# Attention regrouped, and 40 unused products ahead of the first transposes, in a chain of attention and two gated layers

## The chip, the core and the metric

One core of a Trainium2 chip. The time is the device time of one execution in microseconds (us); 0.2% of it, 3.4 us, is about what a measurement of this kernel can tell from no change. The engines are TensorE (PE for its products, PEld for the loading of its stationary operand), VectorE (DVE), ScalarE (ACT), GpSimd (POOL) and SyncE (SP), which issues all DMAs here. Each engine takes its instructions in the order in which the program lists them.

## The reference

```
kv  = einsum('bhsd,bhse->bhde', k, v)             # 8 batches, 8 heads, 576 tokens, 64
out = einsum('bhsd,bhde->bhse', q, kv)
x   = out / sqrt(mean(out*out, -1) + 1e-6) * g_norm   # to 4608 tokens x 512
x   = (sigmoid(x @ w_gate) * (x @ w_val)) @ w_out     # inner width 1536
x   = elu(x @ w_in) @ w_out2                          # inner width 2048
```

All is f32. The attention has no softmax: a 64 x 64 product of k and v per batch and head, and then q times it.

## The kernel before

**Blocks.** The 4608 tokens are cut into 12 blocks of 384 (three chunks of 128), and a batch has 576 tokens, so the border between two batches falls into the middle of a block in every third block (1, 4, 7, 10), and there one of its three chunks of 128 is split into two of 64. Blocks go in pairs (g = 0 to 5).

**Precision.** An f32 operand is split into a high and a low part (fp32r), and a product is three: high x high, high x low, low x high (matmul3, lines 425 to 427). The weights come from memory as raw 64-bit words and are decoded once: `decode` (line 279) loads two pieces of raw (512 KB each, line 288), works on them with ACT (290, 292) and DVE (294, 298), and then ACT writes the high part into a tile S (342) and DVE the low part (344). S, high and low, and the words (wf) are stored for later blocks.

**Attention of a block** (`attention`, line 458). If a batch is new, `kv_batch` (437) loads k and v in four pieces of 512 KB and a tail of 256 KB, multiplies them on PE (451, 453), and ACT copies the results into kvb (455). Then two tasks, each for two pairs of heads, multiply q with kvb (481); ACT squares (488), DVE sums up (489), 13 small DVE operations compute the inverse root (497 to 504), and DVE scales (516, the normalisation, four operations). PE transposes the result (526, four tasks of three), ACT writes the high part of x (533) and DVE the low part (534).

**First layer.** For blocks 0 and 1 `in1_plain` (618) makes, for a pair of inner tiles fp, four groups of 12 products: g for e = 0 and 1, v for e = 0 and 1. The calls are plain(0, 0), plain(1, 0), plain(0, 1), plain(1, 1), where the first number is fp and the second the block; then the other fp. Later pairs of blocks use a scheme with seven products in place of eight on sums and differences (`quad`, line 561); there the attention of the next pair is merged into the products of the present one.

**Second layer.** `in2` (685), and then the output: `out2_plain` (696) for the first pair of blocks, whose six results go through four tiles xp and from there to memory, and `out2` (716) for the five other pairs. `out2` first makes the differences T1, T2, T3 (`combine`, 723), eight operations each on POOL, and T4 on DVE; its products split each operand into a tile J with ACT (644) and DVE (646).

**What sets the order.** The PE order is written by hand (`plan.pe` and the lists `later`). All other work is put in order by a planner (`Plan`, line 60), which plays the program with its own costs and gives each engine the work that is due next; buffers come from pools of fixed size (`slots`: five S, three raw, four wk, three kv, one tail, four xp, 48 v, and eight product banks, psi and psa). A DMA that is issued waits for the one that was issued eight before.

The start before: attention of block 0, then the products of batch 1's k and v (line 818), then the transposes of block 0, then plain(0, 0) with block 1's attention products between its g and v groups, plain(1, 0), the transposes of block 1, plain(0, 1).

The functions that the diff touches:

Of the kernel before, what the change touches and what calls it, by code (L numbers as in the profile page):

```python
# [9 lines left out]
F32 = mybir.dt.float32  # L10
# [11 lines left out]
P = 128  # L22
# [4 lines left out]
BLK = 384  # L27
# [195 lines left out]
def tile_kernel(ctx: ExitStack, tc: tile.TileContext, kv, kvtail, qt, g2, w1, w2, out):  # L223
# [213 lines left out]
    def kv_batch(b, queue, first=False, bank="psa"):  # L437
        tl = plan.buf("tail")
        ld_t = dma(P * 2048, lambda: nc.sync.dma_start(out=tl.slot, in_=kvtail[b]), bufs=[tl], early=30.0)
        for p in range(NP):  # L440
            t, view, ld = load_kv(b, p, "wk" if first and p > 1 else "kv")
            pb = plan.buf(bank)

            def mm(t=t, view=view, pb=pb, p=p):

                k, r = view(), slice(p % 2 * D, p % 2 * D + D)
                for c in range(SC + 1):
                    for h in range(2):
                        e = slice(h * D, h * D + D)
                        if c < SC:  # L450
                            nc.tensor.matmul(pb.slot[e, :D], k[:, 0, c, e], k[:, 1, c, e], start=(c == 0), stop=False)  # L451
                        else:
                            nc.tensor.matmul(pb.slot[e, :D], tl.slot[r, p // 2, 0, e], tl.slot[r, p // 2, 1, e], start=False, stop=True)
            m = add("PE", 0.98, mm, [ld, ld_t], [t, tl, pb], queue=queue)
            kvdone[b, p] = [add("ACT", 0.2, lambda pb=pb, p=p, e=slice(h * D, h * D + D): nc.scalar.activation(
                kvb[b % 2][e, p, e], pb.slot[e, :D], AF.Copy), [m] + kvread.get((b - 2, p), []), [pb]) for h in range(2)]

    def attention(j, queue, direct=None, bank="psa", gap=3, hold=None):
# [8 lines left out]
        for pp in range(NP // 2):  # L467
            qs, lds = [], []
            for p in (2 * pp, 2 * pp + 1):
                qb = plan.buf("v", "q")  # L470
                lds.append(dma(P * BLK * 4, lambda qb=qb, p=p: nc.sync.dma_start(out=qb.slot, in_=qt[j, p]), bufs=[qb], early=30.0))
                qs.append(qb)
            o, x = [plan.buf(bank) for _ in range(2)], plan.buf("xp")

            def mm(qs=qs, o=o, pp=pp):

                for k in range(2):
                    for i in range(TPB):
# [4 lines left out]
            m = add("PE", 0.9, mm, lds + sum((kvdone[b, p] for b in bs for p in (2 * pp, 2 * pp + 1)), []), qs + o, queue=queue)  # L483
# [30 lines left out]
        for pp in range(NP // 2):  # L514
            for h in range(2):
                norm[pp, h] = add("DVE", T_DVE, lambda x=xn[pp], o=po[pp][h], pp=pp, h=h: nc.vector.tensor_tensor(
                    x.slot[:, h, :].rearrange("q (n d) -> q n d", d=D), o.slot[:, :BLK].rearrange("q (n d) -> q n d", d=D),
                    small(2)[:, 2 * pp + h, :].unsqueeze(2).to_broadcast([P, 2 * TPB, D]), op=ALU.mult), last, [xn[pp], po[pp][h], sm])
        for p in range(NP):
            x, n = xn[p // 2], [norm[p // 2, p % 2]]  # L520
            tp = plan.buf("psa")

            def tr(x=x, tp=tp, p=p):
                v = x.slot[:, p % 2, :].rearrange("q (i n) -> q i n", n=P)
                for i in range(TPB):
                    nc.tensor.transpose(tp.slot[:, i * P:(i + 1) * P], v[:, i, :], ident)  # L526
            m = add("PE", 0.35, tr, n, [x, tp], queue=queue)
            if direct is None:
                f = plan.buf("v", "xf")
                res.append((f, add("ACT", T_ACT, lambda f=f, tp=tp: nc.scalar.activation(f.slot, tp.slot[:, :BLK], AF.Copy, scale=gcol), [m], [tp, f])))  # L530
            else:
                f, c = direct[p // 2], p % 2
                hi = add("ACT", T_ACT, lambda f=f, c=c, tp=tp: nc.scalar.activation(f.slot[:, c, 0, :], tp.slot[:, :BLK], AF.Copy, scale=gcol), [m], [tp, f])
                res.append((f, [hi, add("DVE", T_DVE, lambda f=f, c=c, tp=tp: nc.vector.scalar_tensor_tensor(  # L534
                    f.slot[:, c, 1, :], tp.slot[:, :BLK], gcol, f.slot[:, c, 0, :].bitcast(F32), op0=ALU.mult, op1=ALU.subtract), [hi], [tp, f])]))
        return res


# [76 lines left out]

        return {(0, 0): res["11"], (0, 1): res["12"], (1, 0): res["21"], (1, 1): res["22"]}

    def in1_plain(fp, blk, sg, dg, sv, dv, xs, dx, between=()):

        res = {}  # L620
        banks = {(w, e): plan.buf("psi") for w in "gv" for e in range(2)}
# [1 line left out]
        for w, s, d in (("g", sg, dg), ("v", sv, dv)):  # L623
            for e in range(2):
# [71 lines left out]
    def out2_plain(g, hs):  # L696
        acc = {blk: [plan.buf("psi" if blk == 0 else "psa") for _ in range(TPB)] for blk in range(2)}
        for f in range(NF2):
            if f % 2 == 0:
                s, ld = stream("O", f // 2)  # L700
            for blk in in_blocks(f, NF2):
                j, dj = split(*hs[f // 2][f % 2, blk])
                for i in range(TPB):
# [3 lines left out]
                                *v, f == 0, f == NF2 - 1)  # L707
                    t = add("PE", 3 * MMW, mm, ld + dj, [acc[blk][i], s, j])
                    if f == NF2 - 1:
                        e = plan.buf("xp")  # L710
                        view = lambda e=e: e.slot.rearrange("q a n -> q (a n)")[:, :DM]
                        c = copy_out(i, view, lambda b=acc[blk][i]: b.slot, [t], [e, acc[blk][i]])
                        r0 = (2 * g + blk) * BLK + i * P
                        dma(P * 2048, lambda view=view, r0=r0: nc.sync.dma_start(out=out[r0:r0 + P, :], in_=view()), [c], [e], due=0.5)

    def out2(g, hs):
# [6 lines left out]
        def combine(x, y, dst=None, eng="POOL"):  # L723
            res = []
            for i, ((a, da), (b, db)) in enumerate(zip(x, y)):
                d = dst[i][0] if dst else plan.buf("w")
                e, t = (nc.gpsimd, T_POOL) if eng == "POOL" else (nc.vector, T_DVE)
                t = add(eng, t, lambda e=e, d=d, a=a, b=b: e.tensor_tensor(d.slot, a.slot, b.slot, op=ALU.subtract),
                        [da, db] + used.get(d, []) + ([] if dst else [gate]), [d, a, b])
                for x in {a, b} - {d}:  # L730
                    used.setdefault(x, []).append(t)
# [92 lines left out]
    hs = [{} for _ in range(NF1 // 2)]  # L824
    xa, xb = [X0["x11"], X0["x21"]], [X0["x12"], X0["x22"]]

    def plain(fp, blk, between=()):
# [91 lines left out]
```

## Time and profile before

| | us |
|---|---|
| median of 3 runs | 1685.37 (1684.62 to 1686.62) |
| the profiled execution | 1685.98 |
| its span | 1684.2 |
| PE busy in it | 1657.7 |
| DVE, ACT, POOL busy | 1106.6, 813.4, 334.4 |

PE has almost no idle time in the middle of the kernel. In the first 100 us it is idle for 12.6 us, and the granted clock of TensorE is 0.95 on average there; in the rest it is at 1.00. A row of the timeline gives start, duration, engine, line, operation, what it writes and reads by the program's names without buffer numbers, the number of instructions, and in brackets the idle time before the first of them and what ended it.

### The profile page before, as it was taken

To read this page: it belongs to the slowest core of one execution; us is meant where nothing else is said; L and a number is where in the kernel's file an instruction comes from. 1 tells how busy PE (TensorE), PEld (TensorE's weight loads), DVE (VectorE), ACT (ScalarE), POOL (GpSimd) and SP (SyncE) were. 2 spreads that over 40 slices of the span, in tenths; PEclk is the share of its full clock that TensorE was granted. 3 is DMA by queue.
4 is the path that set the end of the run, shared out by engine and by line. 5 is a ranking of instruction groups with operands and counts; after the bars stand their busy time and mean duration, and the time that the engine had idled before them with its cause. 6 is when DMAs were issued, how large, how long until landed. Compare 5 with 4: busy or idle time off the path is not lost.

```text
span 1684.2 us, 28777 instructions
## 1 busy us (share of the span) xinstructions
PE 1657.7 (98%) x10759; PEld 1622.3 (96%) x10759; DVE 1106.6 (66%) x2054; ACT 813.4 (48%) x1663; POOL 334.4 (20%) x326
## 2 busy tenths in 40 slices
PE   8899999999999999999999999999999999999998
PEld 6899999999999999999999998899999999999998
DVE  5769467655764674567356688678678578568575
ACT  5556333543532343335235465456456456456454
POOL 0001355311311230122021000050140240330320
PEclk9999999999999999999999999999999999999999
DMA  8998887889778778776788899988778778778774
GB/s 318 333 314 297 325 309 273 319 295 327 266 248 291 287 272 291 276 256 244 244 303 330 284 341 334 323 287 296 249 279 285 255 266 297 253 267 290 252 266 161
DMA packets 134332, 480.04 MB, mean 285 GB/s; under 512 B 12080, under 2 KB 60720, under 8 KB 106032
## 3 DMA queue, kind: packets, MB, share of 16 engines
q1 hardware_dynamic: 134192, 478.20, 80.4%
q8 instruction: 85, 1.39, 0.3%
q14 instruction: 55, 0.45, 0.1%
HBM read 393.22 MB, written 84.93 MB: 284 GB/s over the span
## 4 chain that ended last, share of the span: by engine, by line
PE 95%; DVE 2%; DMA 1%; issue 1%; ACT 0%; SPq 0%; DVEq 0%
PE psi L425 21%; PE psi L426 21%; PE psi L427 21%; PE psi L755 4%; PE psi L753 4%; PE psi L754 4%; PE psa L426 4%; PE psa L427 4%; PE psa L425 4%; PE psa L481 2%; PE psa L754 2%; PE psa L753 2%; PE psa L755 2%; PE psa L451 1%; PE psa L526 1%
## 5 line engine op out<-in xcount | busy, mean ns | idle before, releaser
L577 DVE TENSOR_TENSOR v<-v,psi 128x384 f32<-128x384 f32 x540 | 297.5, 552 | 228.8 <-PE psi L427 217.8
L425 PE MATMUL psi<-x,S 128*128 128x384 f32 x1056 | 359.4, 340 | 3.0 <-DVE v L577 2.8
L427 PE MATMUL psi<-x,S 128*128 128x384 f32 x1056 | 354.5, 336 | 4.1 <-DVE S L344 4.1
L426 PE MATMUL psi<-x,S 128*128 128x384 f32 x1056 | 354.3, 335 | 0.2 <-DVE x L534 0.2
L644 ACT ACTIVATE J<-v 128x384 fp32r<-128x384 f32 x336 | 175.1, 523 | 234.2 <-PE psa L427 80.0
L646 DVE TENSOR_TENSOR J<-v,J 128x384 fp32r<-128x384 f32 x336 | 205.0, 617 | 126.0 <-ACT J L644 125.0
L425 PE MATMUL psi<-xt,S 128*128 128x384 f32 x648 | 220.0, 340 | 1.4 <-DVE v L577 1.3
L427 PE MATMUL psi<-xt,S 128*128 128x384 f32 x648 | 216.8, 335 | 0.0
L426 PE MATMUL psi<-xt,S 128*128 128x384 f32 x648 | 216.5, 334 | 0.0
L425 PEld LDWEIGHTS psi<-x,S 128*128 128x128 f32 x1056 | 199.3, 189 | 4.9 <-DVE v L577 3.9
L427 PEld LDWEIGHTS psi<-x,S 128*128 128x128 f32 x1056 | 199.0, 188 | 4.5 <-DVE S L344 4.5
L426 PEld LDWEIGHTS psi<-x,S 128*128 128x128 f32 x1056 | 199.1, 189 | 1.0 <-DVE x L534 0.8
L613 POOL TENSOR_TENSOR v<-v,v 128x384 f32<-128x384 f32 x90 | 98.6, 1102 | 392.9 <-DVE v L577 305.8
L755 PE MATMUL psi<-S,J 128*128 128x256 f32 x560 | 159.4, 285 | 5.1 <-DVE J L646 5.1
L753 PE MATMUL psi<-S,J 128*128 128x256 f32 x560 | 158.4, 283 | 0.0
L754 PE MATMUL psi<-S,J 128*128 128x256 f32 x560 | 158.4, 283 | 0.0
L690 ACT ACTIVATE v<-v 128x384 f32<-128x384 f32 x144 | 75.0, 521 | 128.6 <-DVE v L577 128.6
L692 DVE SCALAR_TENSOR_TENSOR v<-v,v 128x384 f32<-128x384 f32 x144 | 87.8, 610 | 58.8 <-ACT v L691 58.8
L425 PEld LDWEIGHTS psi<-xt,S 128*128 128x128 f32 x648 | 121.7, 188 | 3.4 <-DVE v L577 2.7
L426 PEld LDWEIGHTS psi<-xt,S 128*128 128x128 f32 x648 | 121.7, 188 | 0.0
L427 PEld LDWEIGHTS psi<-xt,S 128*128 128x128 f32 x648 | 121.6, 188 | 0.0
L755 PEld LDWEIGHTS psi<-S,J 128*128 128x128 f32 x560 | 107.4, 192 | 6.3 <-DVE J L646 6.1
(153 smaller groups left out, 3336.7 us busy)
## 6 DMA issues: line engine op xcount, KB each, us to landing
S<-wsO SPq DMA_DIRECT2D x78, 1024.0 KB, 6.2
S<-wsI SPq DMA_DIRECT2D x48, 1024.0 KB, 5.3
S<-wso SPq DMA_DIRECT2D x36, 1024.0 KB, 6.3
S<-wsI SPq DMA_DIRECT2D x48, 768.0 KB, 6.0
raw<-w SPq DMA_DIRECT2D x68, 512.0 KB, 6.4
S<-wsg SPq DMA_DIRECT2D x24, 1024.0 KB, 5.3
S<-wsv SPq DMA_DIRECT2D x24, 1024.0 KB, 5.1
S<-wsg SPq DMA_DIRECT2D x30, 768.0 KB, 6.3
```

Source lines behind the costliest of these rows:

```text
L425: nc.tensor.matmul(acc, wh, xh, start=first, stop=False, skip_group_check=more)
L426: nc.tensor.matmul(acc, wh, xl, start=False, stop=False, skip_group_check=more)
L427: nc.tensor.matmul(acc, wl, xh, start=False, stop=last, skip_group_check=more)
L577: return add("DVE", T_DVE, lambda: nc.vector.tensor_tensor(dst.slot, a.slot, bank[k].slot[:, :BLK], op=ALU.add), after, [dst, a, bank[k]])
L613: t = add("POOL", T_POOL, lambda r=r, b=b: nc.gpsimd.tensor_tensor(r.slot, r.slot, b.slot, op=ALU.mult), [d, s], [r, b])
L644: hi = add("ACT", T_ACT, lambda: nc.scalar.activation(j.slot[:, 0, :], f.slot, AF.Copy), [d], [j, f])
L646: lo = add("DVE", T_DVE, lambda: nc.vector.tensor_tensor(j.slot[:, 1, :], f.slot, j.slot[:, 0, :].bitcast(F32), op=ALU.subtract), [hi], [j ...
L690: a1 = add("ACT", T_ACT, lambda e=e, b=b: nc.scalar.activation(e.slot, ps_or_v(b), AF.Relu, scale=-1.0), [d], [e, b])
L692: res[int(n[0]) - 1, int(n[1]) - 1] = (e, add("DVE", T_DVE, lambda e=e, b=b: nc.vector.scalar_tensor_tensor(e.slot, e.slot, -1.0, ps_or_v( ...
L753: nc.tensor.matmul(acc, x[0], w[:, 0], start=st, stop=False, skip_group_check=True)
L754: nc.tensor.matmul(acc, x[0], w[:, 1], start=False, stop=False, skip_group_check=True)
L755: nc.tensor.matmul(acc, x[1], w[:, 0], start=False, stop=last and f == n - 1, skip_group_check=True)
```

## The change

Seven edits, all in the way the same results are computed:

1. The products of batch 1's k and v leave their place ahead of the first transposes and stand among the first block's products: plain(0, 0) has them after its two g groups, block 1's attention products after the first v group; block 1's transposes stand after the first v group of plain(1, 0). Batch 1's fourth piece of k and v goes through four v buffers in four DMAs.
2. 40 products of 256 columns (bf16, of the identity matrix) that nobody reads stand ahead of the first transposes.
3. In an attention task the whole chunks come first, and then the split ones.
4. The transposes are two tasks of six in place of four of three, each after both its normalisations.
5. The third results of out2_plain go through raw and tail in place of xp.
6. In `combine` the last of the eight operations is DVE's.
7. The planner counts 1.4 in place of 0.9 for an attention task on PE.

The core of the diff:

```diff
@@ kv_batch
-            t, view, ld = load_kv(b, p, "wk" if first and p > 1 else "kv")
+            if b == 1 and p > 2:
+                t = [plan.buf("v", "kvx") for _ in range(SC)]
+                chunk = lambda c, t=t: t[c].slot[:, :2 * P].rearrange("q (a n) -> q a n", a=2)
+                ld = [dma(P * 1024, ..., bufs=[t[c]], early=30.0) for c in range(SC)]
...
@@ attention
-                for k in range(2):
-                    for i in range(TPB):
+                whole = [len(spans(j * BLK + i * P, j * BLK + i * P + P)) == 1 for i in range(TPB)]
+                for k, i in [(k, i) for w in (True, False) for k in range(2) for i in range(TPB) if whole[i] == w]:
...
-        for p in range(NP):
-            x, n = xn[p // 2], [norm[p // 2, p % 2]]
-            tp = plan.buf("psa")
+        for pp in range(NP // 2):
+            x, tps = xn[pp], [plan.buf("psa") for _ in range(2)]
...
@@ in1_plain
-            plan.pe += between
-            between = ()
+                plan.pe += between.get(len(t), [])
@@ out2_plain
-                        e = plan.buf("xp")
+                        e, form = ((plan.buf("xp"), ...), (plan.buf("xp"), ...),
+                                   (plan.buf("tail"), ...) if blk else (plan.buf("raw"), ...))[i]
@@ combine
-                e, t = (nc.gpsimd, T_POOL) if eng == "POOL" else (nc.vector, T_DVE)
+                on = "DVE" if i >= n - 1 else eng
+                e, t = (nc.gpsimd, T_POOL) if on == "POOL" else (nc.vector, T_DVE)
@@ the start
-    ra = attention(0, main, [X0["x11"], X0["x21"]], gap=0, hold=later[0])
-    kv_batch(1, main, bank="psi")
-    main += later[0]
+    tr = []
+    ra = attention(0, main, [X0["x11"], X0["x21"]], gap=0, hold=tr)
+    spare = plan.buf("psi")
+
+    def idle_products():
+        z = ident.bitcast(BF16)
+        for _ in range(40):
+            nc.tensor.matmul(spare.slot[:, :256], z[:, :P], z, start=True, stop=True)
+    add("PE", 0.0, idle_products, [], [spare])
+    main += tr
+    kv_batch(1, later[0])
...
-    plain(0, 0, later[1])
-    plain(1, 0)
-    main += later[2]
+    plain(0, 0, {2: later[0], 3: later[1]})
+    plain(1, 0, {3: later[2]})
```

SP's queue at the very start, before (kv, tail and wk hold k and v, v the q tiles here):

```order
L813 DMA gcol_66<-g2 128x1 [waits Activation_49]
L435 DMA kv0_143<-kv 128x1024
L439 DMA tail0_146<-kvtail 128x512
L435 DMA kv1_144<-kv 128x1024
L435 DMA wk0_139<-kv 128x1024
L435 DMA wk1_140<-kv 128x1024
L471 DMA v0_80<-qt 128x384
```

The load of gcol stands first, and the four pieces of k and v in a row. And after:

```order
L435 DMA kv0_143<-kv 128x1024
L439 DMA tail0_146<-kvtail 128x512
L435 DMA kv1_144<-kv 128x1024
L435 DMA wk0_139<-kv 128x1024
L820 DMA gcol_66<-g2 128x1 [waits Activation_49]
L288 DMA raw0_136<-w1 128x1024
L288 DMA raw1_137<-w1 128x1024
L435 DMA wk1_140<-kv 128x1024
L477 DMA v0_80<-qt 128x384 [waits DMAHW0_49]
```

The load of gcol, which waits for ACT, moved behind four loads of k and v, and two raw weight loads stand ahead of the fourth.

DVE's queue around the normalisation of block 0 and the first low halves of x, after (the small operations of lines 503 to 510 are ahead of it; before, lines 294 and 298 stand behind the normalisation, line 516, and line 344 of the first tile stands between them and the low halves, line 534; now both steps of the first tile, S0, stand ahead of the first reduction):

```order
L294 SCALAR_TENSOR_TENSOR wk0_139<-raw0_136,wk0_139 128x512
L522 TENSOR_TENSOR xp0_76<-psa0_153,sm0_147 128x384
L522 TENSOR_TENSOR xp0_76<-psa1_154,sm0_147 128x384
L522 TENSOR_TENSOR xp1_77<-psa2_155,sm0_147 128x384
L522 TENSOR_TENSOR xp1_77<-psa3_156,sm0_147 128x384
L298 SCALAR_TENSOR_TENSOR wk1_140<-wk1_140,wk0_139 128x1024
L540 SCALAR_TENSOR_TENSOR x110_69<-psa0_153,gcol_66,x110_69 128x384
L540 SCALAR_TENSOR_TENSOR x110_69<-psa1_154,gcol_66,x110_69 128x384
```

The decode of the second tile (v of the first pair) has a step ahead of the normalisation and one between it and the low halves.

DVE's queue in the first call of out2, where the last inputs come from in2 (line 692 before, 697 after) and the first product's J (646, now 651) are made, before:

```order
L692 SCALAR_TENSOR_TENSOR v23_103<-v23_103,v10_90 128x384
L646 TENSOR_TENSOR J2_135<-v32_112,J2_135 128x384
L692 SCALAR_TENSOR_TENSOR v40_120<-v40_120,v11_91 128x384
L646 TENSOR_TENSOR J0_133<-v18_98,J0_133 128x384
L646 TENSOR_TENSOR J1_134<-v36_116,J1_134 128x384
L646 TENSOR_TENSOR J2_135<-v16_96,J2_135 128x384
```

And after, with the last operations of T1, T2 and T3 (line 735):

```order
L697 SCALAR_TENSOR_TENSOR v33_113<-v33_113,v41_121 128x384
L651 TENSOR_TENSOR J2_135<-v8_88,J2_135 128x384
L735 TENSOR_TENSOR kv0_143<-v33_113,v45_125 128x384
L697 SCALAR_TENSOR_TENSOR v40_120<-v40_120,v32_112 128x384
L651 TENSOR_TENSOR J0_133<-v36_116,J0_133 128x384
L735 TENSOR_TENSOR kv0_143<-v18_98,kv0_143 128x384
L651 TENSOR_TENSOR J1_134<-v5_85,J1_134 128x384
L735 TENSOR_TENSOR v33_113<-v18_98,v33_113 128x384
L651 TENSOR_TENSOR J2_135<-v43_123,J2_135 128x384
```

One combination stands ahead of the second of these J (J0) and one ahead of each of the two that follow.

## Rows read from the trace of the kernel before

**Rows 1.** The page: shares of the chain that ended last, by engine.

```profile
PE 95%; DVE 2%; DMA 1%; issue 1%; ACT 0%; SPq 0%; DVEq 0%
```

**Rows 2.** Stretches: us, busy time (instructions) by engine, granted clock, DMA share, GB/s.

```profile
0.00:6.50 6.50, 3.17 (x7) 0.89 (x7) 1.30 (x4) 1.49 (x2) 0.70 (x6) 1.00 0.39 126
6.50:13.40 6.90, 5.99 (x81) 4.91 (x81) 0.00 (x0) 1.31 (x6) 0.00 (x0) 1.00 1.02 384
...
18.30:21.00 2.70, 2.70 (x61) 2.23 (x60) 2.27 (x10) 1.36 (x5) 0.00 (x0) 1.00 1.04 416
21.00:25.00 4.00, 0.00 (x0) 0.00 (x0) 3.72 (x11) 3.81 (x8) 0.00 (x0) 0.94 0.89 335
25.00:29.00 4.00, 3.96 (x33) 3.73 (x33) 3.38 (x5) 2.42 (x6) 0.00 (x0) 0.50 0.79 268
...
48.40:51.80 3.40, 3.40 (x12) 3.40 (x11) 1.91 (x4) 1.55 (x2) 0.00 (x0) 0.50 1.01 343
58.50:100.00 41.50, 41.33 (x250) 40.91 (x249) 32.20 (x56) 25.97 (x46) 0.00 (x0) 1.00 0.91 331
160.00:200.00 40.00, 40.00 (x233) 40.00 (x232) 22.64 (x36) 17.77 (x30) 8.86 (x11) 1.00 0.96 365
```

**Rows 3.** Timeline, the first instructions of ACT and SP's issues.

```profile
0.73 1.28 ACT L801 ACT_TABLE_LOAD   x1 [0.73 <-PEq L912]
...
2.25 0.39 SPq L813 DMA_DIRECT2D gcol<-g  x1
...
14.36 1.46 SPq L288 DMA_DIRECT2D raw<-w  x3
```

**Rows 4.** Timeline of PE and DVE, 13 to 59 us.

```profile
13.40 4.97 PE L481 MATMUL psa<-kvb,v 128*128 128x128 f32 x24
...
22.19 1.95 DVE L516 TENSOR_TENSOR xp<-psa,sm 128x384 f32<-128x384 f32 x4
24.05 1.28 DVE L294 SCALAR_TENSOR_TENSOR wk<-raw,wk 128x512 int32<-128x512 int32 x2
25.44 1.23 DVE L298 SCALAR_TENSOR_TENSOR wk<-wk,wk 128x1024 int32<-128x1024 int32 x1
...
28.93 2.19 DVE L534 SCALAR_TENSOR_TENSOR x<-psa,gcol,x 128x384 fp32r<-128x384 f32 x4
...
34.50 4.20 PE L481 MATMUL psa<-kvb,v 128*128 128x128 f32 x32
38.46 0.42 PE L425 MATMUL psi<-x,S 128*128 128x384 f32 x1
...
44.24 1.95 DVE L516 TENSOR_TENSOR xp<-psa,sm 128x384 f32<-128x384 f32 x4
...
47.37 0.44 PE L427 MATMUL psi<-x,S 128*128 128x384 f32 x1 [4.14 <-DVE S L344]
...
57.04 1.47 PE L526 MATMUL psa<-ident,xp 128*128 128x128 f32 x12
58.27 0.42 PE L425 MATMUL psi<-x,S 128*128 128x384 f32 x1
```

**Rows 5.** Stretches of line 481 alone: a task with split chunks, one without.

```profile
226.44:228.38 1.94, 1.94 (x16) 1.36 (x16) 1.00 1.05 350
77.55:78.81 1.26, 1.26 (x12) 1.26 (x12) 1.00 1.04 416
```

**Rows 6.** Timeline of DVE and PE at the end of out2_plain.

```profile
1081.49 0.69 DVE L651 COPY xp<-psa 128x512 f32<-128x512 f32 x1 [4.57 <-DMA out<-xp]
...
1084.38 0.44 PE L425 MATMUL psi<-x,S 128*128 128x384 f32 x1 [2.56 <-DVE v L577]
```

**Rows 7.** Waits of PE, 1100 us on (total, times, longest); timeline at one of them.

```profile
PE psi L755 <- DVE J L646: 5.1, 5, 1.0
...
1619.57 1.03 POOL L728 TENSOR_TENSOR wk<-v,v 128x384 f32<-128x384 f32 x1 [3.31 <-DVE v L692]
1619.61 1.40 DVE L646 TENSOR_TENSOR J<-v,J 128x384 fp32r<-128x384 f32 x1
...
1625.21 0.56 DVE L646 TENSOR_TENSOR J<-v,J 128x384 fp32r<-128x384 f32 x1 [0.69 <-ACT J L644]
```

More of the change, by code (lines that the diff above doesn't have):

```diff
@@ L440, in kv_batch, with mm @@
         for p in range(NP):
-            t, view, ld = load_kv(b, p, "wk" if first and p > 1 else "kv")
+            if b == 1 and p > 2:
+                t = [plan.buf("v", "kvx") for _ in range(SC)]
+                chunk = lambda c, t=t: t[c].slot[:, :2 * P].rearrange("q (a n) -> q a n", a=2)
+                ld = [dma(P * 1024, lambda c=c, chunk=chunk: nc.sync.dma_start(out=chunk(c), in_=kv[b, p][:, :, c, :]), bufs=[t[c]], early=30.0) for c in range(SC)]
+            else:
+                t, view, ld = load_kv(b, p, "wk" if first and p > 1 else "kv")
+                t, ld, chunk = [t], [ld], lambda c, view=view: view()[:, :, c, :]
             pb = plan.buf(bank)
-            def mm(t=t, view=view, pb=pb, p=p):
-                k, r = view(), slice(p % 2 * D, p % 2 * D + D)
+            def mm(chunk=chunk, pb=pb, p=p):
+                r = slice(p % 2 * D, p % 2 * D + D)
                 for c in range(SC + 1):
@@ L450, in mm @@
                         if c < SC:
-                            nc.tensor.matmul(pb.slot[e, :D], k[:, 0, c, e], k[:, 1, c, e], start=(c == 0), stop=False)
+                            nc.tensor.matmul(pb.slot[e, :D], chunk(c)[:, 0, e], chunk(c)[:, 1, e], start=(c == 0), stop=False)
                         else:
                             nc.tensor.matmul(pb.slot[e, :D], tl.slot[r, p // 2, 0, e], tl.slot[r, p // 2, 1, e], start=False, stop=True)
-            m = add("PE", 0.98, mm, [ld, ld_t], [t, tl, pb], queue=queue)
+            m = add("PE", 0.98, mm, ld + [ld_t], t + [tl, pb], queue=queue)
             kvdone[b, p] = [add("ACT", 0.2, lambda pb=pb, p=p, e=slice(h * D, h * D + D): nc.scalar.activation(
@@ L482, in mm @@
                                              kvb[b % 2][:, 2 * pp + k, :], start=True, stop=True)
-            m = add("PE", 0.9, mm, lds + sum((kvdone[b, p] for b in bs for p in (2 * pp, 2 * pp + 1)), []), qs + o, queue=queue)
+            m = add("PE", 1.4, mm, lds + sum((kvdone[b, p] for b in bs for p in (2 * pp, 2 * pp + 1)), []), qs + o, queue=queue)
             for b in bs:
@@ L518, in attention @@
                     small(2)[:, 2 * pp + h, :].unsqueeze(2).to_broadcast([P, 2 * TPB, D]), op=ALU.mult), last, [xn[pp], po[pp][h], sm])
-        for p in range(NP):
-            x, n = xn[p // 2], [norm[p // 2, p % 2]]
-            tp = plan.buf("psa")
[L523 to L535, printed above, removed]
@@ new lines, in attention, with tr @@
+        for pp in range(NP // 2):
+            x, tps = xn[pp], [plan.buf("psa") for _ in range(2)]
+            def tr(x=x, tps=tps):
+                for n, tp in enumerate(tps):
+                    for i in range(TPB):
+                        nc.tensor.transpose(tp.slot[:, i * P:(i + 1) * P], x.slot[:, n, i * P:(i + 1) * P], ident)
+            m = add("PE", 0.62, tr, [norm[pp, 0], norm[pp, 1]], [x] + tps, queue=queue)
+            for c, tp in enumerate(tps):
+                if direct is None:
+                    f = plan.buf("v", "xf")
+                    res.append((f, add("ACT", T_ACT, lambda f=f, tp=tp: nc.scalar.activation(f.slot, tp.slot[:, :BLK], AF.Copy, scale=gcol), [m], [tp, f])))
+                else:
+                    f = direct[pp]
+                    hi = add("ACT", T_ACT, lambda f=f, c=c, tp=tp: nc.scalar.activation(f.slot[:, c, 0, :], tp.slot[:, :BLK], AF.Copy, scale=gcol), [m], [tp, f])
+                    res.append((f, [hi, add("DVE", T_DVE, lambda f=f, c=c, tp=tp: nc.vector.scalar_tensor_tensor(
+                        f.slot[:, c, 1, :], tp.slot[:, :BLK], gcol, f.slot[:, c, 0, :].bitcast(F32), op0=ALU.mult, op1=ALU.subtract), [hi], [tp, f])]))
@@ L709, in out2_plain @@
                     if f == NF2 - 1:
[L710 to L711 removed]
+                        e, form = ((plan.buf("xp"), "q a n -> q (a n)"), (plan.buf("xp"), "q a n -> q (a n)"),
+                                   (plan.buf("tail"), "q a b n -> q (a b n)") if blk else (plan.buf("raw"), "q a b -> q (a b)"))[i]
+                        view = lambda e=e, form=form: e.slot.bitcast(F32).rearrange(form)[:, :DM]
                         c = copy_out(i, view, lambda b=acc[blk][i]: b.slot, [t], [e, acc[blk][i]])
@@ L825, in tile_kernel, with plain @@
     xa, xb = [X0["x11"], X0["x21"]], [X0["x12"], X0["x22"]]
-    def plain(fp, blk, between=()):
+    def plain(fp, blk, between={}):
         r, xs = (ra, xa) if blk == 0 else (rb, xb)
```

4 lines of the change are left out of this document (2 added, 2 removed).

## The prediction

> **What bounds the kernel now.** I read the chain of waits by engine first: TensorE (PE) stands on 95% of it [rows 1]. So time is gained only where PE stands still, runs at its lower clock, or does work that needn't be done. The table of stretches then says where that is. In 160 to 200 us PE is never idle and a product of 384 columns takes 40.00/233 = 0.172 us; the first 58 us look otherwise: nothing at all on PE in 21 to 25 us, a granted clock of 0.50 in 25 to 29 us and again in 48.4 to 51.8 us [rows 2]. Loads run at 384 GB/s from 6.5 us on. The timeline names the second gap: at 47.37 PE had waited 4.14 us for the low half of a decoded weight tile (S, line 344) [rows 4], which stands on VectorE (DVE) behind the whole normalisation of the second block. Last, the waits of the later stages: one of 2.56 us at 1084 us [rows 6], and five of 1.0 us, one in each of the five last output stages [rows 7].
>
> **1. The start, up to the first product of plain(0, 1), which stands at 58.27 us [rows 4].** Before, the first load waits behind that of gcol, issued at 2.25, when ScalarE's (ACT) table load from 0.73 and its first instruction are over [rows 3]. Now four loads stand ahead of gcol and wait for nothing, so the stream can begin at about 0.75, 1.5 to 1.9 us earlier. But two raw weight loads (1 MiB) stand ahead of the fourth kv load. By an estimate from the rates of [rows 2], 0.82 MB are there at 6.5 and 384 GB/s follow; up to the fourth kv load it is now 3.41 MB, which is 13.25 less 1.9 = 11.4 us, and with the q loads 4.19 MB, 13.4 us; loads that are open together finish out of turn, for which I add 0 to 1.3 us. The fourth kv product costs twice the 0.88 us that a step has at full clock (2.70 us for three [rows 2]). So the first block's attention products start between 13.4 (as before [rows 4]) and 14.7; I take 14.1, 0.7 later than before.
>
> From there every step is moved by 0.7: the products (4.97 us) end at 19.0, and the four normalisations, which began at 22.19, could begin at 22.9. Now DVE has one decode step in front of them (half of 1.28, so 0.64): 23.5; they take 1.95, to 25.4; another decode step (1.23) ends at 26.6, and the four low halves of x follow in steps of 2.19/4 = 0.55 [rows 4]: 27.2 to 28.8. The idle products (40 of 256 columns, by columns 256/384 of 0.172 = 0.115 us each, 4.6 us in all) run from 19.0 to 23.6 while PE would wait anyway; the transposes can start after two normalisations at 24.4. If they run at the lower clock for some time they end later, but up to about 25.6 the decode step in front of the low halves covers it; 9.2 us, all of them at half clock, would cost 2.6. The transposes themselves (12, 1.23 us at full clock) are hidden under DVE too. The weight chain for the first product no longer bounds: its raw loads, issued at 14.36 before [rows 3], are now the sixth and seventh of the stream, and its DVE steps stand ahead of the first reduction.
>
> First product of the first weight pair: held by the low halves, done two products after 28.8, 29.15. Then PE has no reason to wait: second product group 12 x 0.172 = 2.06, 31.2; the kv products that stood in the gap now cost 4 x 0.88 and a little for entering, 3.6, 34.8; third group 36.9; attention of block 1, 3.96 before (34.50 to its end 38.46) and 0.5 less by the regrouping below, 40.4; fourth 42.5; three groups of the second weight pair 48.7; 12 transposes 49.9; the last group 52.0. The moved kv products bring seven loads with them; the tail's waits in SP's queue for the last products of batch 0, as it did before, and by the counting of bytes (7.6 MB) all are there at 24, before 31.2. Their copies on ACT stand among decode steps of 0.5 to 1.1 us and are wanted at 36.9, two us after the last. Is the weight there in time? The second pair's first tile was 4.14 us late because DVE took the normalisation first; in the order of after it stands ahead of the second reductions, and by the same counting is ready near 37, five us before 42.5. The normalisation of block 1 came 44.24 + 1.95 - 38.46 = 7.7 us after the attention products; now 48.1, just ahead of 48.7. Result: 58.27 - 52.0 = **6.3 us** gained. Bounds: 7.5 with loads as early as they can be; 2.0 with two stretches at half clock (below), the normalisation a us late, and a later decode late by 1 to 2, for loads run at a share of 0.91 in 58 to 100 us [rows 2] and everything now asks for them earlier.
>
> At one place the Trainium skill speaks against the idle products. The row first: 25 to 29 us holds kv products and the first transposes, and the granted clock stayed at 0.50 (1.2 GHz) to its end although PE was busy for 3.96 of 4.00 us [rows 2]. The Trainium skill, TensorE: Matmul & The Clock Gate, section Part 4: PE-mode transpose, says that transposes do not count as PE being busy as other products do; by it the transposes after the idle products would not hold the clock up, and the sum would be the rival "clock" below. The row agrees with it, but the clock had already fallen there; that it falls in such a place no row shows.
>
> **2. Regrouped attention products.** Only blocks with a split chunk change: 1, 4, 7, 10. A task with two split chunks takes 1.94 us and one without takes 1.26 [rows 5], so a split chunk costs 0.34 more than a whole one. Now both split chunks stand together, and one entry and one exit go. Bounds 0 and 0.34 a task; I take 0.25, since the products themselves remain. Six tasks outside the start: **1.5 us** (0 to 2.0). Transposes in pairs issue the same instructions; nothing is to be had there, since PE does not wait at them in the middle of the kernel.
>
> **3. Copies at the end of out2_plain.** Six copies into four xp tiles: DVE's copy waited 4.57 us for a store out of xp, DVE's later sums stood behind it, and PE waited 2.56 us for one of them [rows 6]. With raw and tail as third targets no copy waits for a store. Tail is loaded no more by then, and of raw's three tiles the sums of the output weights, off PE's path, want one; the sum that PE waited for can follow its products at once, and nothing else is seen late there: **2.6 us** (0 to 2.7).
>
> **4. The last combination of each three on DVE instead of POOL.** Five times PE waits 1.0 us for a low half J [rows 7]. The rows say why: beside a POOL operation (1619.57, 1.03 us) DVE's step on two such tiles takes 1.40 us; without one it takes 0.56 [rows 7]. Three POOL operations follow each other there, the last of T1, T2 and T3, and three DVE steps are so lengthened by some 0.84 each, 2.5 us, the last of them the J that PE waits for. In the order of after these three are on DVE, at 0.56, and only one stands ahead of that J: it ends 2.5 - 0.56 = 1.9 us earlier, against a wait of 1.0. I take **4.7 us** of 5.1; if POOL were not the cause, DVE has 0.56 more in front of that J, five times, a loss of 2.8.
>
> **Sum.** 6.3 + 1.5 + 2.6 + 4.7 = 15.1 us off the profiled execution's own 1685.98 (span 1684.2 and 1.8 around it): 1670.9. The median of the runs is 0.6 lower than that execution, so 1670.3 us.
>
> **The rivals.**
> Clock: PE falls to 1.2 GHz between the idle products' end (23.6) and the steady products (27.2). For: PE had 4.00 us without work in 21 to 25 and stood at 0.50 afterwards; against: here the gap is 27.2 - 23.6 = 3.6 us. Price: 3.40 us at half clock hold 12 products instead of 20 [rows 2], 1.4 us; two such stretches 2.8. Time 1673.1.
> Combination without effect: DVE, not POOL, is what is full where J is late; the three operations fill what is freed. For: DVE has no idle time in front of the late J. Against: the 1.40 beside the 0.56. Gain 0 instead of 4.7, 1675.0; at worst 1677.8.
> Slower: the weights cannot follow the denser products. Place: DVE's and ACT's decode queue from the second weight pair to the end of the first layer's plain stage. A late tile costs what it cost at 47.37, 4.14 us, and 1.4 for the clock that fell at 48.4: 5.5 each. It takes four late tiles to outweigh 15.1 (22 us, 1692). For: loads near their limit. Against: PE was idle for only 41.50 - 41.33 us in 58 to 100 with the same weights.
>
> **How the numbers follow.** Forecast 0.58, clock 0.20, combination 0.14, slower 0.06; 0.02 that several parts fall short together. The range: 7.5 + 2.0 + 2.7 + 5.1 with about 2 us of other small waits is 19.3, 1666; at the other end the combination fails at its worst, 1677.8, and the start falls a little short: 1678.5. I put the low end at 1665.5. A measurement of this kernel can tell 0.2% (3.4 us) from no change; by the cases the chance of faster is 0.90, of no change 0.04, of slower 0.06.
>
> **What would show it.** First load issued before 1 us; no PE wait for a kv load after 18 us; plain(0, 1) starting near 52; no wait for S line 344 on PE; the clock at 1.0 from about 20 us on; split tasks near 1.69 us; no wait for out<-xp on DVE; no wait of 1.0 us for J in the five output stages, and DVE's J at 0.56 there. I am wrong if PE stands still for a weight between 30 and 100 us, or if the five waits for J are still there.

## The result, and the profile after

The changed kernel takes 1667.09 us (median of 4 runs, 1666.79 to 1668.83), the kernel before beside it 1685.32 (1684.62 to 1686.62): a ratio of 0.9894 with a 95% interval of 0.9878 to 0.9909, 18.2 us less. A second measurement of the same kernel, beside the last experiments, gave 1667.06 and 0.9886 (0.9873 to 0.9900). The profiled execution has a span of 1665.0 us in place of 1684.2. The forecast of 1670.3 was 3.2 us too long, its sign and its order of the parts right.

The chain by engine on the page of the changed kernel, and all waits of TensorE that its trace lists (engine, tile, line, what it waited for: us in total, times, longest):

```profile
PE 97%; DVE 2%; DMA 1%; SPq 0%; issue 0%; ACT 0%; DVEq 0%
```

```profile
PE psa L457 <- DMA wk<-kv: 2.3, 1, 2.3
PE psi L816 <- DVE v L814: 2.3, 1, 2.3
PE psi L425 <- DVE v L583: 1.5, 4, 0.5
PE psi L426 <- DVE x L540: 0.9, 1, 0.9
PE psa L531 <- DVE xp L522: 0.6, 1, 0.6
PE psa L457 <- DMA kv<-kv: 0.3, 1, 0.3
```

PE now stands on 97% of the chain, against 95% [rows 1]. The five waits for J [rows 7] and the wait for a weight at line 344 [rows 4] are not in the list any more, and nothing new took their place: the largest that can still be moved is the first, for a kv load at 12.54 us.

The same stretches as in [rows 2], of the changed kernel:

```profile
0.00:6.50 6.50, 4.20 (x25) 1.87 (x25) 1.30 (x4) 1.49 (x2) 0.70 (x6) 1.00 0.66 218
18.30:21.00 2.70, 2.70 (x27) 2.45 (x26) 2.44 (x9) 2.52 (x5) 0.00 (x0) 1.00 1.00 383
21.00:25.00 4.00, 3.44 (x29) 2.62 (x27) 3.76 (x13) 0.71 (x3) 0.00 (x0) 1.00 1.10 365
25.00:29.00 4.00, 3.13 (x19) 2.62 (x18) 4.00 (x6) 3.40 (x7) 0.00 (x0) 1.00 1.05 393
48.40:51.80 3.40, 3.39 (x24) 3.00 (x23) 3.40 (x7) 3.40 (x8) 0.00 (x0) 1.00 0.67 186
58.50:100.00 41.50, 41.50 (x258) 41.18 (x258) 29.29 (x51) 24.58 (x43) 0.00 (x0) 1.00 0.93 335
```

Three things differ. The loads moved 218 GB/s in the first 6.5 us, where it was 126. The granted clock (the number behind the five busy times) is 1.00 in every row, where two rows stood at 0.50. (In the first 17 us or so, here and in [rows 2], that 1.00 is not borne out by the products: 16 kv products at 12.54 us take 1.12 us, as they did before at 25.04 us in the row at 0.50, and 0.69 us at 30.92.) And DVE, the third busy time, is full in 25 to 29 and in 48.4 to 51.8 us, which will matter below.

The timeline of the start (start, duration, engine, line, operation, count, in brackets the idle time before and what ended it):

```profile
0.74 0.40 SPq L435 DMA_DIRECT2D kv<-kv  x1
...
3.17 0.93 SPq L288 DMA_DIRECT2D raw<-w  x2
...
12.54 1.12 PE L457 MATMUL psa<-wk 128*64 128x64 f32 x16 [2.35 <-DMA wk<-kv]
...
14.01 4.80 PE L487 MATMUL psa<-kvb,v 128*128 128x128 f32 x24
...
15.67 1.23 DVE L344 TENSOR_TENSOR S<-wk,S 128x1024 fp32r<-128x1024 f32 x1 [1.12 <-ACT S L342]
...
18.64 4.53 PE L831 MATMUL psi<-ident 128*128 128x256 bf16 x40
...
23.04 1.94 DVE L522 TENSOR_TENSOR xp<-psa,sm 128x384 f32<-128x384 f32 x4
23.74 1.92 PE L531 MATMUL psa<-ident,xp 128*128 128x128 f32 x12 [0.56 <-DVE xp L522]
24.90 1.22 DVE L298 SCALAR_TENSOR_TENSOR wk<-wk,wk 128x1024 int32<-128x1024 int32 x1
26.03 2.19 DVE L540 SCALAR_TENSOR_TENSOR x<-psa,gcol,x 128x384 fp32r<-128x384 f32 x4
26.70 0.44 PE L426 MATMUL psi<-x,S 128*128 128x384 f32 x1 [0.87 <-DVE x L540]
...
34.14 1.23 DVE L344 TENSOR_TENSOR S<-wk,S 128x1024 fp32r<-128x1024 f32 x1 [0.73 <-ACT S L342]
```

These answer to [rows 3] and [rows 4]: the first load at 0.74, the first raw weight loads at 3.17 (14.36 before), the attention products at 14.01 (14.1 was forecast), the normalisation from 23.04 (23.5), the low halves from 26.03 (26.6). The first weight's last step on DVE starts at 15.67, and the second pair's first weight is done at 35.4, long before TensorE wants it (42.05).

To find where the time went I laid the products of both traces side by side, one by one, and took the difference of their starts. It is 6.23 us at the first product of plain(0, 1) (58.27 before, 52.04 now), 7.1 at 210 us, 10.3 at 760 us (six tasks of attention products with split chunks, 0.37 each, and about 1 us more at the transposes and in small waits), 13.0 at the end of the first plain output stage, and then five steps of about 1.2 to 19.0.

### The profile page after: what moved, and what is told of

Its sections match the earlier page's. It is cut to its first block, busy times and chain, and to the rows that moved or that the text cites. A ratio compares the mean times of both kernels' runs of the same rounds, so it can differ in the third digit from the quotient of the medians.

```text
span 1665.0 us, 28863 instructions
## 1 busy us (share of the span) xinstructions
PE 1652.7 (99%) x10799; PEld 1620.9 (97%) x10799; DVE 1101.7 (66%) x2069; ACT 812.1 (49%) x1663; POOL 317.6 (19%) x311
## 3 DMA queue, kind: packets, MB, share of 16 engines
q8 instruction: 85, 1.39, 0.3%
## 4 chain that ended last, share of the span: by engine, by line
PE 97%; DVE 2%; DMA 1%; SPq 0%; issue 0%; ACT 0%; DVEq 0%
PE psi L425 21%; PE psi L426 21%; PE psi L427 21%; PE psi L762 4%; PE psi L761 4%; PE psi L760 4%; PE psa L427 4%; PE psa L426 4%; PE psa L425 4%; PE psa L762 2%; PE psa L761 2%; PE psa L760 2%; PE psa L487 2%; PE psa L457 1%; PE psa L531 1%; DMA wk<-kv 1%
## 5 line engine op out<-in xcount | busy, mean ns | idle before, releaser
L651 DVE TENSOR_TENSOR J<-v,J 128x384 fp32r<-128x384 f32 x336 | 200.9, 601 | 117.8 <-ACT J L649 116.5
L697 DVE SCALAR_TENSOR_TENSOR v<-v,v 128x384 f32<-128x384 f32 x144 | 84.2, 585 | 59.1 <-ACT v L696 58.9
L587 ACT ACTIVATE v<-psi 128x384 f32<-128x384 f32 x108 | 52.3, 484 | 116.5 <-PE psi L427 116.2
```

The lines of the kernel that those rows point to most:

```text
L651: lo = add("DVE", T_DVE, lambda: nc.vector.tensor_tensor(j.slot[:, 1, :], f.slot, j.slot[:, 0, :].bitcast(F32), op=ALU.subtract), [hi], [j ...
L697: res[int(n[0]) - 1, int(n[1]) - 1] = (e, add("DVE", T_DVE, lambda e=e, b=b: nc.vector.scalar_tensor_tensor(e.slot, e.slot, -1.0, ps_or_v( ...
```

## The experiments

The kernel before, run beside the three groups of experiments, took 1684.6, 1685.1 and 1686.7 us (medians); they lie 2.1 us apart, so by its time alone a difference of under about 2 us between kernels of different groups is not told apart from none. The changed kernel itself, measured twice, moved by 0.03 us. Each kernel is the changed one with the edit shown, and differences are to its 1667.1, unless said otherwise.

**Without the idle products.**

```diff
-        for _ in range(40):
+        for _ in range(0):
```

> The changed kernel without the 40 idle products. Theory (they hold the clock): TensorE then has nothing to do for about 5 us (18.6 to 23.7 us), the granted clock falls to 0.5 as it did in the kernel before at 21 to 25 us, and the first products of plain(0, 0) run at half speed for about 3.4 us: 1.4 us longer than the changed kernel by the same count as in the prediction, 2.8 if the transposes at half speed also push DVE's low halves back. So 1668.5 to 1670. Rival (the idle products do nothing, since the low halves of x are what the first products wait for): 0, 1667.1, with a granted clock that either does not fall or falls where TensorE waits anyway.

Measured: 1667.27 us (1666.84 to 1667.80), +0.2. The stretches around the gap, here and with the same columns as above:

```profile
18.90:23.70 4.80, 0.00 (x0) 0.00 (x0) 4.30 (x18) 2.12 (x4) 0.00 (x0) 0.76 1.09 367
23.70:26.20 2.50, 2.42 (x12) 2.45 (x13) 2.50 (x5) 1.40 (x3) 0.00 (x0) 0.50 1.03 390
26.20:28.00 1.80, 1.80 (x7) 1.54 (x6) 1.80 (x4) 1.74 (x3) 0.00 (x0) 0.50 1.08 399
28.00:30.00 2.00, 2.00 (x13) 2.00 (x12) 2.00 (x4) 1.66 (x4) 0.00 (x0) 0.95 1.03 420
```

The theory's mechanism is there: PE does nothing for 4.8 us, the clock falls to 0.50 (1.2 GHz) and comes back at 28 us. Its price is not. DVE's low halves stand where they stood (26.07 us), and the first products had to wait for them anyway; product by product this kernel is 0.7 us behind after six products, 0.3 at 50 us, 0.1 at 1108, and two traces of the changed kernel themselves differ by 0.3 in their first products. The idle products keep the clock up and are worth next to nothing.

**The last combination back on POOL, and the same edit alone on the kernel before.**

```diff
-                on = "DVE" if i >= n - 1 else eng
+                on = eng
```

This is the edit undone; the second kernel is the one before with the same line added.

> The changed kernel with the last combination of each three back on POOL. Theory (POOL's step beside DVE's makes DVE's step on J take 1.40 us in place of 0.56): the five waits of 1.0 us for the low half of J come back, 1.2 us per output stage, in all 5 to 6 us: 1672 to 1673. Rival (the waits went because other edits moved DVE's work before these stages): 0, 1667.1, and no waits of 1.0 us for J on TensorE.

> The kernel before with one edit alone: the last combination of each three on DVE. Theory: the five waits for J go with nothing else changed, 5 to 6 us off 1685.3, that is 1679.3 to 1680.3; TensorE waits no 1.0 us for J and DVE's J step takes 0.56 us. Rival (DVE is what is full there, and the other edits are needed as well): 0 or up to 2.8 us longer, 1685 to 1688.

Measured: 1673.10 us (1672.93 to 1673.96), +6.0, when it is undone; on the kernel before the edit alone gives 1679.97 (1676.52 to 1682.00) against 1684.62, a ratio of 0.9969 (0.9957 to 0.9980), that is 3.4 to 7.2 us less. First the waits of the kernel with the edit undone, from 1100 us, and its timeline at one of them:

```profile
PE psi L762 <- DVE J L651: 5.1, 5, 1.0
```

```profile
1607.67 1.03 POOL L735 TENSOR_TENSOR wk<-v,v 128x384 f32<-128x384 f32 x1 [3.31 <-DVE v L697]
1607.72 1.39 DVE L651 TENSOR_TENSOR J<-v,J 128x384 fp32r<-128x384 f32 x1
...
1611.74 0.39 PE L762 MATMUL psi<-S,J 128*128 128x256 f32 x1 [1.02 <-DVE J L651]
```

And the same place of the changed kernel:

```profile
1602.25 0.55 DVE L735 TENSOR_TENSOR wk<-v,v 128x384 f32<-128x384 f32 x1
1603.22 0.55 DVE L651 TENSOR_TENSOR J<-v,J 128x384 fp32r<-128x384 f32 x1
1603.69 0.55 DVE L735 TENSOR_TENSOR raw<-v,wk 128x384 f32<-128x384 f32 x1
1604.16 0.55 DVE L651 TENSOR_TENSOR J<-v,J 128x384 fp32r<-128x384 f32 x1
```

Beside POOL the step on J takes 1.39 us, alone 0.55. With three more operations DVE is done sooner. Against the rival, the edit works without the others: in the profile of the kernel before with it, the five stages give 9.36 - 3.25 = 6.1 us. The Trainium skill, SBUF — State Buffer, section Who interferes with whom, says that a DVE operation with two inputs in SBUF contends with a GpSimd operation that reads SBUF; the 1.39 beside the 0.55 agree.

**The third copies back in xp.**

```diff
-   (plan.buf("tail"), "q a b n -> q (a b n)") if blk else (plan.buf("raw"), "q a b -> q (a b)"))[i]
+   (plan.buf("xp"), "q a n -> q (a n)"))[i]
```

> The changed kernel with the third copies at the end of the first plain output stage back in xp. Theory: the copy on DVE waits some 4.5 us for a store out of xp again, TensorE waits 2.6 us about 13 us before the next stage, and the time is 2.7 us longer: 1669.8. Rival (the earlier arrival of everything before has moved the copies apart, so the store is over in time): 0, 1667.1.

Measured: 1670.65 us, +3.6, but its four runs are 1666.89, 1670.28, 1671.03 and 1672.03. DVE and PE in its timeline, and the stretch behind the wait:

```profile
1070.51 0.69 DVE L656 COPY xp<-psa 128x512 f32<-128x512 f32 x1 [4.23 <-DMA out<-xp]
...
1073.43 0.44 PE L425 MATMUL psi<-x,S 128*128 128x384 f32 x1 [2.25 <-DVE v L583]
```

```profile
1074.00:1078.00 4.00, 4.00 (x16) 4.00 (x15) 2.55 (x6) 3.16 (x7) 0.00 (x0) 0.57 0.93 304
```

The wait of [rows 6] is back, and behind it the clock fell for some products (16 in 4 us in place of 25), which makes the loss 4.1 us in this trace (product by product, from 0.35 us ahead of the changed kernel to 3.76 behind). In the kernel before, the clock stayed at 1.00 behind the like wait of 2.56 us. How long the store holds xp changes from run to run: in the kernel before with the combination moved PE waited 0.62 us here. One of the four runs of this kernel is as short as the changed kernel; there is no trace of it, so that the store was over sooner in it is not shown. By these runs the edit is worth 0 to 5 us.

**The split chunks in their old places.**

```diff
-   for k, i in [(k, i) for w in (True, False) for k in range(2) for i in range(TPB) if whole[i] == w]:
+   for k, i in [(k, i) for k in range(2) for i in range(TPB)]:
```

> The changed kernel with the split chunks of the attention products in the old places (one per half, each with its own entry and exit). Theory: each of the six tasks with two split chunks takes 0.37 us longer, and the products of block 1 at the start 0.71 longer: 2.9 us, 1670.0, with first-to-next times of 1.94 us per task in place of 1.57. Rival (the tasks are shorter only because their neighbours changed): 0, 1667.1.

Measured: 1669.45 us (1668.89 to 1669.98), +2.4; product by product +2.8 at 690 us. Stretches of the attention products alone (length, busy PE and weight loads, clock, DMA): first the changed kernel, a task with two split chunks and one without, then this kernel.

```profile
222.60:224.17 1.57, 1.57 (x16) 1.28 (x16) 1.00 1.06 436
70.76:72.02 1.26, 1.26 (x12) 1.26 (x12) 1.00 1.04 406
```

```profile
223.28:225.22 1.94, 1.94 (x16) 1.36 (x16) 1.00 0.99 400
```

The same 16 products take 1.57 us in place of 1.94 because the split ones stand together. All six tasks show it to 0.001 us (0.367 each), and block 1 at the start, with 32 products, saves 0.71 (3.25 in place of 3.96). The Trainium skill, TensorEngine Tiling (Array Packing), section Key Properties, says that a change of the tiling mode drains TensorE; these rows fit that and put a number on the change; that the time goes into such a drain no row shows.

**The start in the old order.** In PE's order, the first kernel undoes all of it; the second keeps the idle products, so that the clock stays up, and undoes only the place of the second batch's kv products. The first loads of k and v stay early in both, but the planner follows the order of the products: it issues the first raw weight loads at 8.76 and 9.22 us, where the changed kernel has them at 3.17.

```diff
-    add("PE", 0.0, idle_products, [], [spare])
+    kv_batch(1, main, bank="psi")
...
-    plain(0, 0, {2: later[0], 3: later[1]})
-    plain(1, 0, {3: later[2]})
+    plain(0, 0, {2: later[1]})
+    plain(1, 0)
+    main += later[2]
```

> The changed kernel with the start in the old order: the second batch's kv products in front of the first transposes, no idle products, the attention products of block 1 at their old places. Theory: the start term comes back nearly whole, 5 to 6.5 us (gcol still stands behind four loads, so the loads keep their 1.5 to 1.9 us): 1672 to 1673.5. Rival (the gain at the start came from the loads that are issued earlier, not from the order of products): under 2 us, 1667 to 1669.

```diff
     add("PE", 0.0, idle_products, [], [spare])
+    kv_batch(1, main, bank="psi")
     main += tr
-    kv_batch(1, later[0])
```

> The changed kernel with the second batch's kv products back in front of the first transposes, but with the 40 idle products kept ahead of them. This keeps the clock up and undoes the place alone. Theory (the gain is that the kv products' 3.6 us no longer stand in front of the first transposes, and that products are there to run while the second weight is decoded): first plain product later by 2 to 4 us, 1669 to 1671. Rival (the clock is what counts): 0 to 1 us, 1667.1 to 1668.

Measured: 1673.05 us (1672.16 to 1674.21), +6.0, for the first, and 1672.42 (1671.90 to 1674.27), +5.3, for the second. Of the second, a long stretch, the waits of PE in 28 to 60 us, and its timeline (raw loads, the last step of the first weight and of the second pair's first weight, and the wait for the latter):

```profile
16.00:44.00 28.00, 23.17 (x220) 19.80 (x219) 22.61 (x55) 19.45 (x39) 0.00 (x0) 1.00 0.97 339
```

```profile
PE psi L427 <- DVE S L344: 4.3, 3, 3.0
PE psi L425 <- ACT S L342: 1.9, 2, 1.0
```

```profile
9.22 0.81 SPq L288 DMA_DIRECT2D raw<-w  x2
...
25.88 1.23 DVE L344 TENSOR_TENSOR S<-wk,S 128x1024 fp32r<-128x1024 f32 x1 [1.12 <-ACT S L342]
...
43.77 1.22 DVE L344 TENSOR_TENSOR S<-wk,S 128x1024 fp32r<-128x1024 f32 x1
...
44.91 1.94 DVE L522 TENSOR_TENSOR xp<-psa,sm 128x384 f32<-128x384 f32 x4
...
45.04 0.44 PE L427 MATMUL psi<-x,S 128*128 128x384 f32 x1 [2.99 <-DVE S L344]
```

The clock stayed at 1.00 for these 28 us, and still nearly the whole term came back, more than the theory gave (2 to 4 us). So the clock in the gap ahead of the transposes is not where the gain comes from. The waits for line 344 of [rows 4] return, but not because PE's 3.5 us of kv products are missing: PE comes to the second pair's first weight at 41.54 us, 0.5 earlier than in the changed kernel (42.05), and the weight is done at 45.0 in place of 35.4. With the raw loads 6 us later, the first weight's last step starts at 25.88 in place of 15.67, and DVE works for 8.71 us in 5 to 25 us in place of 11.31. These two kernels therefore undo the order of the products together with the earlier weights that the planner makes of it, and what each of the two is worth alone was not tried. Behind the late weights the clock did fall (0.50 in 46.2 to 49.5 and in 53.0 to 56.3 us): 18 products came at steps of 0.32 us in place of 0.17, about 2.6 of the 7.5 us by which this trace, of the slowest of five runs, is longer.

**gcol first in the load queue.**

```diff
-    dg = dma(512, lambda: nc.sync.dma_start(out=gcol, in_=g2))
+    dg = dma(512, lambda: nc.sync.dma_start(out=gcol, in_=g2), due=-50.0)
```

> The changed kernel with the load of gcol put back at the front of the load queue, so that all loads again wait for ScalarE's table load and first instruction; every other order is the same. Theory of the prediction (the loads' 1.5 to 1.9 us pass on to the first product): 1668.6 to 1669. Rival (the undoing of the order of products alone already cost 5.9 of 6.2 us, so the earlier loads bring almost nothing; DVE's work bounds the start): 0 to 0.5 us, 1667.1 to 1667.6.

Measured: 1668.24 us (1667.73 to 1668.63) beside 1667.06 of the changed kernel in the same group, +1.2. Its first kv load is issued at 2.71 in place of 0.74 us; the first product comes 1.5 us later. The prediction's theory holds, at somewhat less than its size; the rival (0 to 0.5) falls. Together with the order of the products and the weights that follow it (5.3 to 6.0) this is 6.5 to 7.2, around the 6.2 to 6.8 that all gave together.

> The changed kernel once more, as it is, so that small differences of the two beside it can be read on the same chip: 1667.1, within 0.7 us.

Measured: 1667.06 us (1666.64 to 1668.05).

**Two attempts to win more at the start.** The first puts the four kv loads ahead of gcol and the raw loads, and two decode steps of the second weight behind the low halves of x; the second puts the four kv loads and the four q loads ahead of them.

```diff
-  ... bufs=[t], early=30.0)
+  ... bufs=[t], early=30.0, due=-50.0 if cls == 'wk' or b == 0 else None)
...
-  op0=ALU.bitwise_and, op1=ALU.bitwise_or), [b], [raw, wp])
+  op0=ALU.bitwise_and, op1=ALU.bitwise_or), [b] + (behind if behind and n else []), [raw, wp])
```

> The changed kernel with two things in another order at the start: all four kv loads of the first batch ahead of gcol and the raw weight loads, and the last two decode steps of the second weight (lines 294 and 298) behind the normalisation and the low halves of x on DVE. Theory: in the changed kernel TensorE waited 2.35 us at 12.54 us for the fourth kv load, and two decode steps of 0.68 and 1.22 us stand in front of the low halves; both go, DVE's reductions begin 1.5 to 2.3 us earlier and the low halves end 1.5 to 3 us earlier: 1664 to 1665.6. Rival (the raw loads are then late, and the weight's steps take the place of the wait): 0 or up to 2 us longer, 1667 to 1669.

```diff
-  ... in_=qt[j, p]), bufs=[qb], early=30.0)
+  ... in_=qt[j, p]), bufs=[qb], early=30.0, due=p - 40.0 if j == 0 else None)
```

> The changed kernel with all four kv loads and the four q loads of block 0 ahead of gcol and the raw weight loads; the normalisation then stands ahead of most of the decode steps on DVE. Theory: the attention products start at about 11.5 us in place of 14.0 and the low halves of x end 1.5 to 3 us earlier, and what is won stays if no weight of the first two pairs is late: 1664 to 1666. Rival (DVE has no free time before 50 us, so that every step put forward makes a weight or the second block's normalisation late, as with the four kv loads and the low halves put forward: 0.87 us earlier at the first products, 1.29 later at 50 us): 0 or up to 3 us longer, 1667 to 1670.

Measured: 1667.73 us (1667.30 to 1670.41), +0.6, and 1674.99 (1673.44 to 1675.86), +7.9. The first did bring the low halves 0.9 us forward, and at 50 us is 1.3 behind: the second block's normalisation had been pushed back, and the transposes waited for it. The second, in its timeline and two stretches:

```profile
11.94 5.18 PE L487 MATMUL psa<-kvb,v 128*128 128x128 f32 x24
...
25.44 0.42 PE L425 MATMUL psi<-x,S 128*128 128x384 f32 x1
...
52.17 0.69 PE L425 MATMUL psi<-x,S 128*128 128x384 f32 x1 [4.19 <-ACT S L342]
```

```profile
21.50:26.90 5.40, 2.31 (x14) 1.57 (x15) 5.40 (x9) 3.24 (x6) 0.00 (x0) 1.00 0.94 260
27.00:30.00 3.00, 3.00 (x11) 3.00 (x11) 2.90 (x6) 1.29 (x3) 0.00 (x0) 0.50 0.98 373
48.00:52.00 4.00, 0.00 (x0) 0.00 (x0) 4.00 (x7) 3.10 (x5) 0.00 (x0) 0.85 0.77 313
```

Its attention products start 2.1 us earlier and its first weight product at the same time (25.44 against 25.41), since DVE is busy for all of 21.5 to 26.9 us; then the second pair's second weight is 4.2 us late, with DVE again full and PE idle. In the first kernel the rival's time holds. In the second the rival is right that a weight comes late, but not in its price (0 to 3 us) nor in that DVE has no free time: its raw loads are issued at 7.85 us in place of 3.17, DVE is idle for 11.9 us before 14.14, and in 5 to 25 us it works for 8.62 us in place of 11.31. So DVE's work on the weights sets the start, and the order of the loads sets when DVE can begin it. No version here is faster than the changed kernel.

## Why the prediction was right

**The start: 6.3 forecast, 6.23 measured** at its own mark, the first product of plain(0, 1) (52.0 forecast, 52.04). The steps between are within 0.6 us of the text: attention products 14.01, normalisation 23.04, low halves from 26.03, kv products 30.92, block 1's attention 36.61. Two products later the lead is 6.8. The text held that PE would not wait for the second pair's first weight, since that weight stands ahead of the second reductions on DVE and is ready near 37; it was ready at 35.4 (47.3 before), and in both kernels in the old order, where it is ready at 45.0, PE waits again. What the text did not separate is how the 6.2 divide: 5.3 to 6.0 for the order of the products with the earlier weights that follow from it, 1.2 for the first loads, next to nothing for the idle products. The 0 to 1.3 us for loads that "finish out of turn" no run shows: in both traces the first fourteen loads land in the order in which they were issued. The fourth load of k and v let PE go on at 12.54, 1.1 after the 11.4 of the count, so the size fits; its reason is open.

**Split chunks: 1.5 forecast, 2.2 measured** outside the start (6 x 0.367), and 0.71 in place of 0.5 inside it. The mechanism was right and the term "I take 0.25" mis-sized; 0.367 even lies outside its bound of 0.34. The bound took what one split chunk costs more than a whole one and gave a grouping the chance to save at most that much. By the rows above two split chunks cost 1.94 - 1.26 = 0.68 us apart and 1.57 - 1.26 = 0.31 together: more than half of the price is the change of form, and standing together removes it. The 0.31 left stands at the entry and the exit, for by the starts of the products the second and the third pair of half products step 0.11 us each, as a whole product does.

**Copies: 2.6 forecast, 2.7 between the two traces.** The mechanism is right: DVE has no wait for a store there any more. That the size fits so well is in part luck, for by the runs with the copies undone it is 0 to 5, as the store's time varies.

**Last combination: 4.7 forecast, 6.0 measured** (five steps of about 1.2 between the traces; 6.0 when undone). The mechanism, POOL's step lengthening DVE's, is shown; the term was mis-sized by taking the waits of 1.0 us as all that could be won. Each of the five places gave about 1.2: after a wait the next product too takes longer (0.39 us, against a mean of 0.28 for its kind); this is 0.1 of the 0.2, and the rest is open. DVE's steps at 0.55 also leave it no part of the wait, where I had kept some.

**Transposes in pairs: nothing forecast, 0.9 us between the traces.** The reason given, that the same instructions are issued and PE does not wait at them, overlooked that a group of them costs the products around it something too. By the starts of the products, three transposes lengthen the seven steps around them by 0.353 us and six by 0.661, which is 0.045 less for each of the 20 pairs outside the start. This was not tried by itself, nor were the planner's 1.4 for an attention task and the four v buffers. The parts that were undone (6.0, 1.2, 6.0, 2.4, and 0 to 5 for the copies) add up to 15.6 to 20.6 us, around the 18.2 of the whole.

**Small waits.** Of the 3.2 us won between 210 and 760 us, 2.2 are the split chunks and 0.7 the transposes; the rest are waits of under 0.6 us each, of which the sum had nothing (the range did).

**The rivals.** The clock did not fall: it stands at 1.00 from before the idle products on. The transposes at 23.74 to 25.66, with a wait on either side, did not bring it down, so what the Trainium skill says of transposes in TensorE: Matmul & The Clock Gate, Part 4, had no effect here that a row shows. Its price was also wrong: with the clock down (no idle products) the loss was 0.2 us, not 1.4 to 2.8, because DVE's low halves were the later of the two. In the kernel with the q loads first it did fall after the same 40 products (0.50 in 27 to 30 us), PE having been busy for 2.31 of 5.40 us: the rival's mechanism exists, in a place that this kernel does not have. The rival "combination without effect" is refuted by both runs of that edit. The slower one, weights that cannot follow denser products, did not come: PE was busy for 41.50 of 41.50 us in 58.5 to 100, and its list of waits has none for a weight. But its place was well chosen, for late weights at 45 to 52 us are what the old order and the q loads first were slowed by.

## What to carry to other kernels

Before moving work forward to fill a gap, ask which engine will be waited for next, and what the move does to the loads and steps that this engine needs: here 3.5 us of products done as early as possible cost 5.3 us, with the raw loads 6 us and the weights some 10 us later behind them. Where one engine's operations lengthen another's (1.39 us in place of 0.55 here), try giving the short operations in front of a critical step to the engine that makes the critical step, even if it is the busier one. Put products of the same form next to each other, the split ones among them, and, by the traces, transposes too.

## What the runs showed of the hardware

A change between products of whole chunks (128 tokens) and of half chunks (64), in and out once, costs 0.367 us, the same to 0.001 us in six places. A clock that had fallen in a gap of 4.8 us came back at 28 us, PE having been busy again from 23.78 on, and cost no more than 0.7 us, since PE would have waited for DVE in the first of that time anyway. Behind a wait of 2.25 us the granted clock fell in one trace (0.57 in 1074 to 1078 us, PE having been busy for 1.75 of the 4 us up to the end of the wait), and behind one of 2.56 us, with PE busy for 1.44 of the 4 us up to its end, it stayed at 1.00 in another. A store out of the same tiles held a copy for 4.57, 4.23 and 2.64 us in three traces of otherwise equal stages.
